# A 2-D Fourier transform feeding a SwiGLU block: another split gate, two moved ScalarE units and one later VectorE step

## The chip, the core and the metric

The kernel runs on one core of one Trainium2 chip, as one launch. The metric is the device time of one execution in microseconds (us), lower is better. A profiled execution gives a trace beside it: when each instruction of each engine started and ended. TensorE is called PE there, VectorE DVE, ScalarE ACT, GpSimd POOL and SyncE SP.

## The reference

```python
X = np.fft.fft(x, axis=1)          # x: (8, 3008, 256) float32
X = np.fft.fft(X, axis=2)
y = X.real.reshape(8 * 3008, 256)
g = y @ w_gate                     # 256 x 1536
silu = g * (1.0 / (1.0 + np.exp(-g)))
out = (silu * (y @ w_val)) @ w_out # 1536 x 256, out (24064, 256)
```

Only the real part of the transform is wanted, and x is real. So the rows k and 3008 - k of one batch come from the same two parts, one even in k and one odd: row k is even + odd, the mirrored row 3008 - k is even - odd.

## The kernel before

**Tiles and units.** The transform along the sequence gives for each batch 1504 columns of an even part (tile `Pt`) and of an odd part (`Qt`), 128 rows each; the transform along the 256 features has been multiplied into the weights at the start (`Wp` for the even part, `Wq` for the odd one, and `Wm`, which is -2 times `Wq` with its row 0 set to zero). The 12032 columns are cut into 24 tiles (`wide`: 480, 512 and 512 twice, then 512, the last one 320 and 8 columns more). A tile has 12 units, one for each 128 of the 1536 hidden columns; unit 5 of tile 17 is written (17,5). One loop (lines 1045 to 1082) runs over all 288 units, and the order in it is the order on every engine: the schedule is written out by hand, and each engine works through its own list in order.

**A unit.** The gate of the rows k is `Wp`·`Pt` + `Wq`·`Qt` in a PSUM bank g, the value the same with the value's weights in a bank v. For the mirrored rows the gate gets a third product, `Wm`·`Qt`, on top in the same bank (line 907), once ScalarE has read the bank for the first silu (`sg`, line 868). For the value, nearly all units are "split" (`split`, line 788): between the two products VectorE takes a copy `es` of the even half (line 874), and forms the mirrored value as 2·es - v (line 888, tile `VV`). Row 0 of `Qt` does not change its sign; `es` therefore has the term `bc`·`w0` in it, where `bc` is that row spread over all partitions. VectorE multiplies silu and value of the rows k (`hp`, line 882), GpSimd those of the mirrored rows (`hm`, line 912), except in units named by `on_v` (line 792), where VectorE forms the mirrored value in place (line 885) and multiplies too (line 916).

**Seeded units.** In the units of `SEED`, 1, 3 and 10, `es` costs VectorE nothing: ScalarE writes `bc`·`w0` into the v bank ahead (`seed`, line 802, instruction at line 809), the even product is added on top, ScalarE copies the sum to `es` (line 872), and the odd product uses `Wz` (`Wq` with row 0 set to zero). The seed of unit f + 1 is issued in the iteration of unit f.

**Gated units.** In the units of `GATED`, 2, from tile 4 on, the gate is split as the value is: `gate_even` (line 814) issues the even product one iteration ahead, VectorE takes `eg` = even half + `bc`·`w0` (line 823), `gate_odd` (line 827) adds the odd product and takes the silu, and one iteration later VectorE writes 2·eg - g into the bank (line 835). The product with `Wm` is not made in such a unit. There is one buffer for `eg` (`egp`, line 690).

**An iteration.** For unit u the loop issues, in this order: `part_a` (the gate's two products, the value's even product, the silu, `es`); the seed of the next unit; the waiting 2·eg - g; four of the output products (`owork`, line 770, 128x256 each, 96 to a tile, of the tile before); `gate_even` of the next unit if it is gated; `odd` of the unit before (its odd value product, `hp`, `VV`); `part_b` of the unit before (its product with `Wm`, the silu of the mirrored rows, `hm`); `gate_odd`; the copies of finished outputs to `EV` (line 730); four more output products. There are three g banks and three v banks, taken in turn, so unit f + 3 writes the bank of unit f.

**Transforms in between.** In two units of about two tiles in three (units 4 and 6, `job_at`) half of a `transform` (line 607) follows at the end of the iteration: it takes one v and one g bank aside, and VectorE writes the sums to later tiles' `Pt` and `Qt` (line 652). GpSimd folds the input for it until about tile 20. `bc` of the next tile is stored at unit 7 and loaded by DMA on SP's queue at unit 9 (lines 1032 to 1040).

```python
GATED = (2,)
SEED = (1, 3, 10)
return u[1] in ON_V.get(u[0], (8,) if u[0] < LIGHT else ())   # on_v; LIGHT = 14
return u[0] >= 4 and u[1] in GATED and split(u)               # gated
```

Of the kernel before, what the change touches and what calls it, by code (L numbers as in the profile page):

```python
# [14 lines left out]
BF16 = mybir.dt.bfloat16  # L15
AF = mybir.ActivationFunctionType
Alu = mybir.AluOpType
# [14 lines left out]
def kernel(  # L32
# [8 lines left out]
    nc = tc.nc  # L41
    B, M, D = x.shape
    Dff = moe_w_gate.shape[1]
    P = 128
# [4 lines left out]
    nF = Dff // P  # L49
    T = 512  # L50
# [23 lines left out]
    const = ctx.enter_context(tc.tile_pool(name="const", bufs=1))  # L74
# [26 lines left out]
    Wm = const.tile([P, 2, Dff], BF16, name="Wm")  # L101
# [1 line left out]
    Tab = const.tile([P, 2, 2, 2, NTAB], BF16, name="Tab")  # L103
    halfpi = const.tile([P, 1], F32, name="halfpi")
    zero = const.tile([P, 1], F32, name="zero")
    GATED = (2,)
    w0 = const.tile([P, nF + len(GATED)], F32, name="w0")
    sel = const.tile([P, P], BF16, name="sel")
    CD = const.tile([P, 2, P], BF16, name="CD")
    SDt = const.tile([P, 2, P], BF16, name="SDt")  # L110
# [1 line left out]
    mM = const.tile([P, 4], F32, name="mM")  # L112
    wC = const.tile([P, 1], F32, name="wC")
    sgn = const.tile([P, 1], F32, name="sgn")
    SEED = (1, 3, 10)
    Wz = const.tile([P, len(SEED), P], BF16, name="Wz")
    XA = const.tile([P, 8, 2, D], F32, name="XA")
    XC = const.tile([P, 8, 2, D], F32, name="XC")
    CEs = {(nm, i): const.tile([P, 2, 2, 3 * P + 1], BF16, name=f"CE{nm}{i}") for nm in "ac" for i in range(2)}
# [8 lines left out]
    Wraw = [EVw[:, i * 4 * T:(i + 1) * 4 * T].rearrange("p (n f) -> p n f", n=2) for i in range(2)]  # L128
# [123 lines left out]
    W0 = [tp.tile([P, 2, T], BF16, name=f"W0{i}") for i in range(2)]  # L252
# [52 lines left out]
    for i in range(6):  # L305
        ps = psO.tile([P, T], F32, name="o")
# [178 lines left out]
    def value_rows(fcs):  # L485

        n = T // P
        ps = psO.tile([P, T], F32, name="o")
        for fc in fcs:
            src = W0[1] if fc == 0 else Wraw[1][:, :, (fc - 1) * T:fc * T]  # L490
            for f in range(n):
                for no in range(2):
                    nc.tensor.matmul(ps[:, fc * n + f:fc * n + f + 1], src[:, no, f * P:(f + 1) * P],
                                     SDt[:, no, 0:1], start=(no == 0), stop=(no == 1))
        nc.scalar.copy(w0[:, fcs[0] * n:(fcs[-1] + 1) * n], ps[:, fcs[0] * n:(fcs[-1] + 1) * n])
        for k, f in enumerate(GATED):
            if f // n in fcs:
                src = W0[0] if f < n else Wraw[0][:, :, (f // n - 1) * T:f // n * T]
                for no in range(2):
                    nc.tensor.matmul(ps[:, nF + k:nF + k + 1], src[:, no, f % n * P:(f % n + 1) * P],  # L500
                                     SDt[:, no, 0:1], start=(no == 0), stop=(no == 1))
                nc.scalar.copy(w0[:, nF + k:nF + k + 1], ps[:, nF + k:nF + k + 1])

    psA = place(XA, putA, 4, ((psG, "g"), (psV, "v")))
    sums(SA, XA, psA)
# [37 lines left out]
    def angles_o(ch):  # L543
        t1 = rrO[:, ch].bitcast(I32)
        return [lambda i=i: vstt(rrO[:, ch, i, :], kfO, mM[:, 2 * ch + i:2 * ch + i + 1], t1[:, i, :],
                                 op0=Alu.mult, op1=Alu.subtract) for i in range(2)] + [
                lambda: magnitude(raO[:, ch], rrO[:, ch])]
# [235 lines left out]
    ON_V = {1: (6,), 2: (2, 9), 3: (2, 9)}  # L783
    LIGHT = 14

    bc = {}

    def split(u):

        return u[1] not in WHOLE.get(u[0], ())  # L790

    def on_v(u):

        return u[1] in ON_V.get(u[0], (8,) if u[0] < LIGHT else ())

    def gated(u):

        return u[0] >= 4 and u[1] in GATED and split(u)

    seeded = {}  # L800

# [12 lines left out]
    def gate_even(u):  # L814
# [6 lines left out]
        eg = egp.tile([P, T], F32, name="eg")  # L821
        k = nF + GATED.index(f)
        nc.vector.scalar_tensor_tensor(eg[:, :n], bc[t][:, :n], w0[:, k:k + 1], g[:, :n], op0=Alu.mult, op1=Alu.add)
# [11 lines left out]
        mirrored[u] = lambda: nc.vector.scalar_tensor_tensor(g[:, :n], eg[:, :n], 2.0, g[:, :n], op0=Alu.mult,  # L835
                                                             op1=Alu.subtract)

    def part_a(u):
        t, f = u
        n = width(t)  # L840
        w = n + (B if t == nT - 1 else 0)
        fs = slice(f * P, (f + 1) * P)
        if f == 0:
            hts[t] = (hp.tile([P, nF, T + B], BF16, name="hp"), hp.tile([P, nF, T], BF16, name="hm"))
        Pt, Qt = pq_tiles(t)

        def mm(ps, Wt, gv, src, start, stop):
            nc.tensor.matmul(ps[:, :w], Wt[:, gv, fs], src[:, :w], start=start, stop=stop,  # L848
                             skip_group_check=True)

        if gated(u):
            g, sg, _ = gates[u]
        else:
            g = psG.tile([P, T], F32, name="g")
            mm(g, Wp, 0, Pt, True, False)
            if u == (0, 0):
                v = psV.tile([P, T], F32, name="v")
                mm(v, Wp, 1, Pt, True, False)
            mm(g, Wq, 0, Qt, False, True)
        if split(u):  # L860
            mine = u in seeded
            e = seeded.pop(u) if mine else psV.tile()
            mm(e, Wp, 1, Pt, not mine, False)
            if not mine:
                psV.begun[id(e)] = w
            if not gated(u):
                sg = sgp.tile([P, T], F32, name="sg")
                nc.scalar.activation(sg[:, :w], g[:, :w], AF.Silu)  # L868
            stt = nc.vector.scalar_tensor_tensor
            es = next_es()  # L870
            if mine:
                nc.scalar.copy(es[:, :n], e[:, :n])  # L872
            else:
                stt(es[:, :n], bc[t][:, :n], w0[:, f:f + 1], e[:, :n], op0=Alu.mult, op1=Alu.add)  # L874

            def odd():
                if mine:
                    nc.tensor.matmul(e[:, :w], Wz[:, SEED.index(f), :], Qt[:, :w], start=False, stop=True,  # L878
                                     skip_group_check=True)
                else:  # L880
                    mm(e, Wq, 1, Qt, False, True)
                nc.vector.tensor_tensor(hts[t][0][:, f, :w], sg[:, :w], e[:, :w], op=Alu.mult)  # L882
                if on_v(u):
                    vm = e
                    stt(e[:, :n], es[:, :n], 2.0, e[:, :n], op0=Alu.mult, op1=Alu.subtract)
                else:
                    vm = next_of(VV, "vv")
                    stt(vm[:, n - 1::-1], es[:, :n], 2.0, e[:, :n], op0=Alu.mult, op1=Alu.subtract)  # L888
                state[u] = (g, vm)
            return odd  # L890
        if u != (0, 0):
            v = psV.tile([P, T], F32, name="v")
            mm(v, Wp, 1, Pt, True, False)
        psV.begun[id(v)] = w
        mm(v, Wq, 1, Qt, False, True)
        sg = sgp.tile([P, T], F32, name="sg")
        nc.scalar.activation(sg[:, :w], g[:, :w], AF.Silu)  # L897
        nc.vector.tensor_tensor(hts[t][0][:, f, :w], sg[:, :w], v[:, :w], op=Alu.mult)
        state[u] = (g, v)
# [29 lines left out]
    for b in range(2, B, 2):  # L929
        u = slot[(b, 0)] - 1  # L930
# [65 lines left out]
    job_at = {}  # L996
    for jb in jobs[1:]:
        u = slot[jb]
# [13 lines left out]
    def sine_o(ch):  # L1012
        return [lambda: sine(ch, NOO, NTAB, rrO[:, ch])]

    late = angles_o(1)
    before = {0: late[0:1], 1: weight_unit(1, 0) + late[1:2], 2: weight_unit(1, 1) + cosine_o(0), 3: late[2:3],
              4: weight_unit(2, 0), 5: weight_unit(2, 1) + cosine_o(1), 7: sine_o(0), 8: sine_o(1),
              9: [lambda: weigh(NOO, NTAB), lambda: value_rows((1, 2))],
              11: [lambda k=k, f=f: nc.scalar.activation(Wz[:, k, :], Wm[:, 1, f * P:(f + 1) * P], AF.Copy, scale=-0.5)
                   for k, f in enumerate(SEED)]}  # L1020
    loads = []

    def spread_row0(t):
# [21 lines left out]
    for i, u in enumerate(units):  # L1045
        t, f = u
        if (t, f) == (1, 0):
            spread_row0(t)
        if 0 < t < nT - 1 and f in ROW0:
            (store_row0, load_row0)[ROW0.index(f)](t + 1)  # L1050
        for fn in before.pop(i, ()):
            fn()
        run_loads(i)
        coming = part_a(u)
        if i not in job_at and i + 1 < len(units):
            seed(units[i + 1])
        if prev in mirrored:
            mirrored.pop(prev)()
        if owork:
            owork.run(4)  # L1060
        if i + 1 < len(units) and gated(units[i + 1]):
            gate_even(units[i + 1])
        if odd:
            odd()
        odd = coming
        if prev is not None:
            part_b(prev)
            if u in gates:
                gate_odd(u)
            run_evicts()  # L1070
            if prev[1] == nF - 1:
                owork = OWork(prev[0], hts[prev[0]])
                owork.run(4)
        if owork and not (prev is not None and prev[1] == nF - 1):
            owork.run(4)
        for what, j in fold_at.get(i, ()):
            fold_step(what, j, i)
        for what in act_at.pop(i, ()):
            load_next(what)
        if i in job_at:  # L1080
            transform(*job_at[i])
        prev = u
# [38 lines left out]
```

## Time and profile before

| what | value |
|---|---|
| time, median of 3 executions | 625.55 us (625.27 to 625.73) |
| time of the profiled execution | 625.21 us |
| its span, first to last instruction | 623.3 us |
| PE busy | 610.8 us (98%), 4124 matmuls recorded |
| DVE busy | 575.3 us (92%) |
| ACT busy | 470.8 us (76%) |
| POOL busy | 527.2 us (85%) |

A 128x512 matmul shows as 0.38 us, but the next one starts 0.22 us after it: ends are modelled, so starts are what is to be read on PE. Instructions of DVE and of ACT overlap a little in the same way. A few matmul records are missing; where two starts lie 0.43 apart and no row is between, one product is unseen, not a wait. In the trace's rows, an engine's idle time before an instruction, and what ended it, stands in square brackets.

### The profile page before, as it was taken

To read this page: it belongs to the slowest core of one execution; us is meant where nothing else is said; L and a number is where in the kernel's file an instruction comes from. 1 tells how busy PE (TensorE), PEld (TensorE's weight loads), DVE (VectorE), ACT (ScalarE), POOL (GpSimd) and SP (SyncE) were. 2 spreads that over 40 slices of the span, in tenths; PEclk is the share of its full clock that TensorE was granted. 3 is DMA by queue.
4 is the path that set the end of the run, shared out by engine and by line. 5 is a ranking of instruction groups with operands and counts; after the bars stand their busy time and mean duration, and the time that the engine had idled before them with its cause. 6 is when DMAs were issued, how large, how long until landed. Compare 5 with 4: busy or idle time off the path is not lost.

```text
span 623.3 us, 13287 instructions
## 1 busy us (share of the span) xinstructions
PE 610.8 (98%) x4124; PEld 396.4 (64%) x4190; DVE 575.3 (92%) x1053; ACT 470.8 (76%) x880; POOL 527.2 (85%) x543
## 2 busy tenths in 40 slices
PE   9999999999999999999999999999999999999997
PEld 6446666666666666666666666666666666666686
DVE  7889999999999999999999999999999999999991
ACT  7687868778777787787777877877787778778773
POOL 9997989899899989997997989998799856656661
PEclk9999999999999999999999999999999999999999
DMA  8682442244222253244245111134121111111112
GB/s 226 122 171 77 114 139 84 84 115 138 81 67 86 70 151 108 74 134 127 70 109 149 50 44 55 48 85 139 58 59 37 53 45 42 59 52 44 58 52 77
DMA packets 52981, 55.42 MB, mean 89 GB/s; under 512 B 7504, under 2 KB 44238, under 8 KB 52910
## 3 DMA queue, kind: packets, MB, share of 16 engines
q1 hardware_dynamic: 49726, 52.20, 29.2%
q0 software_dynamic: 3184, 2.36, 2.6%
q8 instruction: 33, 0.54, 0.4%
q14 instruction: 38, 0.31, 0.2%
HBM read 32.22 MB, written 24.67 MB: 91 GB/s over the span
## 4 chain that ended last, share of the span: by engine, by line
PE 87%; DVE 6%; ACT 3%; issue 2%; DMA 1%; SPq 0%; POOL 0%; DVEq 0%; ACTq 0%
PE o L770 37%; PE v L848 18%; PE g L848 15%; PE g L907 8%; PE v L620 2%; PE v L878 2%; DVE hp L882 2%; DVE VV L888 1%; DMA XA<-in_x_dram 1%; PE g L620 1%; ACT EV L730 1%; PE g L819 1%; ACT sg L868 1%; PE g L832 1%; DVE hm L916 1%
## 5 line engine op out<-in xcount | busy, mean ns | idle before, releaser
L912 POOL TENSOR_TENSOR hm<-sgv,VV 128x512 bf16<-128x512 f32 (+2 forms) x258 | 322.7, 1258 | 76.7 <-DVE VV L888 66.2
L911 ACT ACTIVATE sgv<-g 128x512 f32<-128x512 f32 (+2 forms) x258 | 153.7, 596 | 62.3 <-PE g L907 55.9
L882 DVE TENSOR_TENSOR hp<-sg,v 128x512 bf16<-128x512 f32 (+2 forms) x273 | 184.1, 675 | 7.6 <-PE v L848 6.2
L868 ACT ACTIVATE sg<-g 128x512 f32<-128x512 f32 (+2 forms) x253 | 151.5, 599 | 30.9 <-PE g L848 20.9
L770 PE MATMUL o<-Wo,hp 128*128 128x256 bf16 (+2 forms) x1140 | 169.6, 273 | 0.1
L770 PE MATMUL o<-Wo,hm 128*128 128x256 bf16 (+2 forms) x1140 | 169.7, 273 | 0.0
L770 PEld LDWEIGHTS <-hm 128*128 128x128 bf16 (+2 forms) x1140 | 112.0, 98 | 70.4 <-issue 2.5
L770 PEld LDWEIGHTS <-hp 128*128 128x128 bf16 (+2 forms) x1140 | 112.0, 98 | 67.8 <-issue 3.4
L888 DVE SCALAR_TENSOR_TENSOR VV<-SDf,v 128x512 f32<-128x512 f32 (+2 forms) x179 | 120.5, 673 | 0.0
L848 PE MATMUL v<-Pt,Wp 128*128 128x512 bf16 (+2 forms) x288 | 107.9, 375 | 5.2 <-DVE hm L916 0.8
L848 PE MATMUL g<-Pt,Wp 128*128 128x512 bf16 (+2 forms) x268 | 100.7, 376 | 0.1
L907 PE MATMUL g<-Qt,Wm 128*128 128x512 bf16 (+2 forms) x267 | 100.0, 375 | 0.7 <-ACT sg L897 0.7
L874 DVE SCALAR_TENSOR_TENSOR SDf<-bc,w,v 128x512 f32<-128x512 bf16 (+2 forms) x116 | 85.1, 734 | 0.2
L848 PE MATMUL v<-Qt,Wq 128*128 128x512 bf16 (+2 forms) x222 | 83.1, 374 | 0.0
L848 PEld LDWEIGHTS <-Wp 128*128 128x128 bf16 x556 | 54.2, 98 | 41.3 <-issue 7.1
L848 PE MATMUL g<-Qt,Wq 128*128 128x512 bf16 (+2 forms) x205 | 76.5, 373 | 0.0
L874 DVE SCALAR_TENSOR_TENSOR es<-bc,w,v 128x512 f32<-128x512 bf16 (+2 forms) x91 | 66.9, 735 | 0.1
L809 ACT ACTIVATE v<-bc,w 128x512 f32<-128x512 bf16 (+2 forms) x66 | 45.2, 685 | 24.1 <-DVE VV L888 23.7
L730 ACT COPY EV<-o 128x512 f32<-128x512 f32 x90 | 52.8, 586 | 4.8 <-PE o L770 4.8
L888 DVE SCALAR_TENSOR_TENSOR VV<-es,v 128x512 f32<-128x512 f32 (+2 forms) x79 | 53.2, 673 | 0.0
L848 PEld LDWEIGHTS <-Wq 128*128 128x128 bf16 x490 | 47.9, 98 | 8.0 <-issue 0.5
L872 ACT COPY SDf<-v 128x512 f32<-128x512 f32 (+2 forms) x66 | 39.1, 592 | 0.0
(189 smaller groups left out, 642.5 us busy)
## 6 DMA issues: line engine op xcount, KB each, us to landing
out_dram<-EV SPq DMA_DIRECT2D x96, 128.0 KB
XA<-in_x_dram SPq DMA_DIRECT2D x32, 256.0 KB
XA<-in_x_dram SPq DMA_DIRECT2D x112, 64.0 KB
XC<-in_x_dram SPq DMA_DIRECT2D x210, 16.0 KB
XC<-in_x_dram SPq DMA_DIRECT2D x56, 60.0 KB
bc<-row SPq DMA_DIRECT2D x20, 128.0 KB
out_dram<-EV SPq DMA_DIRECT2D x12, 120.0 KB
out_dram<-EV SPq DMA_DIRECT2D x10, 112.0 KB
```

The lines of the kernel that those rows point to most:

```text
L730: nc.scalar.copy(ev[:, 0:len(pair), :], ps[:, 0:len(pair), :])
L770: nc.tensor.matmul(ps[:n, j, :], hts[minus][:, f, c:c + n], Wo[:, f, :], start=(f == 0), stop=(f == nF - 1))
L809: nc.scalar.activation(e[:, :w], bc[t][:, :w], AF.Copy, scale=w0[:, f:f + 1])
L848: nc.tensor.matmul(ps[:, :w], Wt[:, gv, fs], src[:, :w], start=start, stop=stop, skip_group_check=True)
L868: nc.scalar.activation(sg[:, :w], g[:, :w], AF.Silu)
L872: nc.scalar.copy(es[:, :n], e[:, :n])
L874: stt(es[:, :n], bc[t][:, :n], w0[:, f:f + 1], e[:, :n], op0=Alu.mult, op1=Alu.add)
L882: nc.vector.tensor_tensor(hts[t][0][:, f, :w], sg[:, :w], e[:, :w], op=Alu.mult)
L888: stt(vm[:, n - 1::-1], es[:, :n], 2.0, e[:, :n], op0=Alu.mult, op1=Alu.subtract)
L907: nc.tensor.matmul(ps[:, :w], Wm[:, gv, f * P:(f + 1) * P], Qt[:, :w], start=False, stop=True, skip_group_check=True)
L911: nc.scalar.activation(sg[:, w - 1::-1], g[:, :w], AF.Silu)
L912: nc.gpsimd.tensor_tensor(hts[t][1][:, f, :w], sg[:, :w], v[:, :w], op=Alu.mult)
```

## The change

- Unit 0 is gated too from tile 14 on, tile 23 included: ten units. Two more one-column products at the start give its `w0` column, and all such products now stand ahead of the copies of their sums.
- Seeded units are 1, 3, 9 and 11 in place of 1, 3 and 10, in every tile from 1 on (11 not in the last tile, which is not split there). The weights of the fourth take the tile `sel`, free after tile 1 has begun.
- In the iterations that carry half of a transform, `es` of the unit is issued behind `odd` of the unit before, not ahead of it.
- `on_v` names unit 9 in place of 8 in tiles 4 to 13.

```diff
-    GATED = (2,)
+    GATED = (2, 0)
-    SEED = (1, 3, 10)
-    Wz = const.tile([P, len(SEED), P], BF16, name="Wz")
+    SEED = (1, 3, 11, 9)
+    Wz3 = const.tile([P, 3, P], BF16, name="Wz")
+    Wz = [Wz3[:, k, :] for k in range(3)] + [sel]
...
+        more = [(k, f) for k, f in enumerate(GATED) if f // n in fcs]
+        for k, f in more:
+            src = W0[0] if f < n else Wraw[0][:, :, (f // n - 1) * T:f // n * T]
+            for no in range(2):
+                nc.tensor.matmul(ps[:, nF + k:nF + k + 1], src[:, no, f % n * P:(f % n + 1) * P],
+                                 SDt[:, no, 0:1], start=(no == 0), stop=(no == 1))
         nc.scalar.copy(w0[:, fcs[0] * n:(fcs[-1] + 1) * n], ps[:, fcs[0] * n:(fcs[-1] + 1) * n])
-        for k, f in enumerate(GATED):
-            if f // n in fcs:
...
+        for k, f in more:
+            nc.scalar.copy(w0[:, nF + k:nF + k + 1], ps[:, nF + k:nF + k + 1])
...
-        return u[1] in ON_V.get(u[0], (8,) if u[0] < LIGHT else ())
+        return u[1] in ON_V.get(u[0], (9,) if u[0] < LIGHT else ())
...
-        return u[0] >= 4 and u[1] in GATED and split(u)
+        return u[0] >= 4 and u[1] in GATED[:1 if u[0] < LIGHT else 2] and split(u)
...
+    even_sums = []
-    def part_a(u):
+    def part_a(u, later):
...
-                stt(es[:, :n], bc[t][:, :n], w0[:, f:f + 1], e[:, :n], op0=Alu.mult, op1=Alu.add)
+                even_sums.append(lambda: stt(es[:, :n], bc[t][:, :n], w0[:, f:f + 1], e[:, :n], op0=Alu.mult,
+                                             op1=Alu.add))
+                if not later:
+                    even_sums.pop()()
...
-                    nc.tensor.matmul(e[:, :w], Wz[:, SEED.index(f), :], Qt[:, :w], start=False, stop=True,
+                    nc.tensor.matmul(e[:, :w], Wz[SEED.index(f)], Qt[:, :w], start=False, stop=True,
...
+    def seed_weights(k):
+        f = SEED[k]
+        nc.scalar.activation(Wz[k], Wm[:, 1, f * P:(f + 1) * P], AF.Copy, scale=-0.5)
...
-              11: [lambda k=k, f=f: nc.scalar.activation(Wz[:, k, :], Wm[:, 1, f * P:(f + 1) * P], AF.Copy, scale=-0.5)
-                   for k, f in enumerate(SEED)]}
+              11: [lambda k=k: seed_weights(k) for k in range(3)], nF + 2: [lambda: seed_weights(3)]}
...
-        coming = part_a(u)
+        coming = part_a(u, i in job_at)
...
         if odd:
             odd()
+        while even_sums:
+            even_sums.pop()()
```

More of the change, by code (lines that the diff above doesn't have):

```diff
@@ L494, in value_rows @@
                                      SDt[:, no, 0:1], start=(no == 0), stop=(no == 1))
-        nc.scalar.copy(w0[:, fcs[0] * n:(fcs[-1] + 1) * n], ps[:, fcs[0] * n:(fcs[-1] + 1) * n])
-        for k, f in enumerate(GATED):
-            if f // n in fcs:
[L498 to L502, printed above, removed]
+        more = [(k, f) for k, f in enumerate(GATED) if f // n in fcs]
[4 more added lines that the diff above has]
+                                 SDt[:, no, 0:1], start=(no == 0), stop=(no == 1))
+        nc.scalar.copy(w0[:, fcs[0] * n:(fcs[-1] + 1) * n], ps[:, fcs[0] * n:(fcs[-1] + 1) * n])
+        for k, f in more:
+            nc.scalar.copy(w0[:, nF + k:nF + k + 1], ps[:, nF + k:nF + k + 1])
     psA = place(XA, putA, 4, ((psG, "g"), (psV, "v")))
```

## The prediction

> **What bounds the kernel.** I read the page first, then the starts of TensorE's matmuls in the timeline, then, wherever two starts lie further apart than a matmul's pitch, the row that the late one waited for.
>
> ```profile
> span 623.3 us, 13287 instructions
> PE 610.8 (98%) x4124; PEld 396.4 (64%) x4190; DVE 575.3 (92%) x1053; ACT 470.8 (76%) x880; POOL 527.2 (85%) x543
> ```
>
> PE is the bound: it follows its own pitch nearly everywhere, so a product taken away is worth its pitch, and any wait put into PE's list is paid in full. VectorE, 92% busy, is close behind it, so what matters is at which unit it runs late. The start of tile 17 stands for all tiles from 14 on. Three views of it follow: PE, VectorE, ScalarE.
>
> ```profile
> 444.69 0.38 PE L878 MATMUL v<-Qt,Wz 128*128 128x512 bf16 x1
> 448.59 0.38 PE L819 MATMUL g<-Pt,Wp 128*128 128x512 bf16 x1
> 448.81 0.38 PE L848 MATMUL v<-Qt,Wq 128*128 128x512 bf16 x1
> 451.42 0.38 PE L848 MATMUL g<-Pt,Wp 128*128 128x512 bf16 x1
> 451.85 0.38 PE L848 MATMUL v<-Pt,Wp 128*128 128x512 bf16 x1
> ```
> ```profile
> 446.41 0.75 DVE L874 SCALAR_TENSOR_TENSOR SDf<-bc,w,v 128x512 f32<-128x512 bf16 x1
> 447.73 0.68 DVE L888 SCALAR_TENSOR_TENSOR VV<-es,v 128x512 f32<-128x512 f32 x1
> 449.01 0.75 DVE L823 SCALAR_TENSOR_TENSOR eg<-bc,w,g 128x512 f32<-128x512 bf16 x1 [0.60 <-PE g L819]
> 449.68 0.68 DVE L882 TENSOR_TENSOR hp<-sg,v 128x512 bf16<-128x512 f32 x1
> 450.27 0.68 DVE L888 SCALAR_TENSOR_TENSOR VV<-SDf,v 128x512 f32<-128x512 f32 x1
> 452.72 0.69 DVE L835 SCALAR_TENSOR_TENSOR g<-eg,g 128x512 f32<-128x512 f32 x1
> ```
> ```profile
> 446.68 0.69 ACT L809 ACTIVATE v<-bc,w 128x512 f32<-128x512 bf16 x1
> 447.33 0.60 ACT L911 ACTIVATE sgv<-g 128x512 f32<-128x512 f32 x1
> 447.83 0.58 ACT L730 COPY EV<-o 128x512 f32<-128x512 f32 x1
> 450.99 0.69 ACT L809 ACTIVATE v<-bc,w 128x512 f32<-128x512 bf16 x1 [0.89 <-DVE VV L888]
> ```
>
> Pitches, from neighbouring starts: PE 0.216 (448.59 to 448.81); VectorE 0.66 behind an `eg` or `es` (449.01 to 449.68), 0.60 behind `hp` and the like (449.68 to 450.27); ScalarE 0.65 behind a seed, 0.49 behind a silu. A matmul's start to its reader on VectorE is 0.42 (448.59 to 449.01). The row to remember is the last: the seed of (17,3) writes the bank of (17,0), so it waits for `VV` of (17,0), which ends at 450.95; it ends at 451.68, and the even product of unit 3 starts at 451.85, on pitch, with about 0.1 to spare. That such a seed does stop PE when it is late stands in tile 4:
>
> ```profile
> 127.93 0.69 ACT L809 ACTIVATE v<-bc,w 128x512 f32<-128x512 bf16 x1 [1.30 <-DVE VV L888]
> 128.16 0.38 PE L848 MATMUL g<-Qt,Wq 128*128 128x512 bf16 x1
> 128.67 0.38 PE L848 MATMUL v<-Pt,Wp 128*128 128x512 bf16 x1
> ```
>
> The seed ends at 128.62, the product follows 0.05 later at 128.67, where pitch would have it at 128.37: 0.30 lost.
>
> **Part 1, unit 0 gated in tiles 14 to 23.** Gone: ten products with `Wm`, nine of 0.216 and one of 320 columns (0.136): -2.08 us. Added: per tile an `eg` (0.66) and a 2·eg - g (0.60) on VectorE, against one `es` (0.66) saved by the fourth seed. What VectorE does in order, in the clock of the rows above: the new gate product takes 444.69, `eg`(0) starts 0.42 later at 445.11; `hp`(10) 445.77, `VV`(10) 446.37, `es`(0) 446.97, `hp`(11) 447.62, `VV`(11) 448.22 to 448.90. Before, that row was at 447.73 and was followed by 0.60 of idle time, the bracket at 449.01; now the lateness and the new 2·eg - g take it up. The latter also needs the silu of unit 0, which now stands on ScalarE behind the seed of unit 1 (447.08, on the end of `VV`(10) at 447.05) and the mirrored silu of 11 (447.74): 448.23 to 448.82. So 2·eg - g runs from 448.86 to 449.55.
>
> Next comes `eg`(2), and there is one `eg` buffer: it must wait for the end of 2·eg - g, which has just read it. What such a wait for the neighbour costs, the mirrored product in place shows in tile 10:
>
> ```profile
> 267.96 0.69 DVE L885 SCALAR_TENSOR_TENSOR v<-es,v 128x512 f32<-128x512 f32 x1
> 268.76 0.69 DVE L916 TENSOR_TENSOR hm<-sg,v 128x512 bf16<-128x512 f32 x1
> ```
>
> 0.80 from start to start in place of 0.60. The Trainium skill says otherwise (VectorE: DVE Perf Modes, The DRAIN you can't avoid): in a chain of vector operations "the semaphore costs nothing extra here". The row disagrees by 0.20; by the rule each of the ten starts would be 0.20 earlier, a rival below. By the row `eg`(2) starts at 449.65, `hp`(0) 450.31, `VV`(0) 450.91 to 451.59; the seed of 3 follows (0.03) 451.62 to 452.31 and PE's product (0.05) 452.36. On pitch, with one product fewer, PE would be there at 451.63: 0.73 lost in each of tiles 14 to 22, so 0.51 net. A smaller wait before it, for ScalarE's copy `es`(1), lies inside these 0.73. In tile 23 the operands of its own units are 320 columns wide; scaled by columns the chain gives about 0.4. Sum of waits 9 x 0.73 + 0.4 = +7.0.
>
> `bc` is read 1.3 earlier than at 446.41.
>
> ```profile
> 66.83 0.36 SPq L1040 DMA_DIRECT2D bc<-row  x1
> 72.02 0.75 DVE L874 SCALAR_TENSOR_TENSOR SDf<-bc,w,v 128x512 f32<-128x512 bf16 x1
> 438.73 0.35 SPq L1040 DMA_DIRECT2D bc<-row  x1
> ```
>
> Tile 2 reads it 5.2 after its issue without waiting; tile 17 now would 6.4 after. I take 0; the other end, landing only just before 446.41, would be 1.3 per tile. No DMA is added or moved.
>
> **Part 2, `es` behind `odd` in transform iterations.** At unit 4 of tiles 5, 7, 10, 13, 16 and 19 (first and last shown) PE's value product of unit 5 waits for `VV`(3), which has `es`(4) ahead of it; in tile 2 it is longer.
>
> ```profile
> 156.07 0.38 PE L848 MATMUL g<-Qt,Wq 128*128 128x512 bf16 x1
> 156.55 0.38 PE L848 MATMUL v<-Pt,Wp 128*128 128x512 bf16 x1
> 504.79 0.38 PE L848 MATMUL g<-Qt,Wq 128*128 128x512 bf16 x1
> 505.27 0.38 PE L848 MATMUL v<-Pt,Wp 128*128 128x512 bf16 x1
> 81.63 0.39 PE L848 MATMUL g<-Pt,Wp 128*128 128x512 bf16 x1
> 82.59 0.38 PE L848 MATMUL v<-Pt,Wp 128*128 128x512 bf16 x1 [0.57 <-DVE VV L888]
> ```
> ```profile
> 503.28 0.74 DVE L874 SCALAR_TENSOR_TENSOR SDf<-bc,w,v 128x512 f32<-128x512 bf16 x1
> 504.54 0.68 DVE L888 SCALAR_TENSOR_TENSOR VV<-SDf,v 128x512 f32<-128x512 f32 x1
> 510.55 1.33 DVE L652 TENSOR_TENSOR Qt<-g,od 128x160 bf16<-128x160 f32 x7 [0.34 <-PE g L641]
> ```
>
> 0.48 in place of 0.216 is 0.27, six times; tile 2 loses 0.96 - 0.43 = 0.53. The step moves `VV`(3) up by as much as 0.66, so all of it goes: -2.15. `es`(4) then runs about where `VV`(3) was, ends near 505.28, and its reader comes a good 0.3 later. PE being ahead by 0.27 afterwards is covered by the 0.34 that VectorE idles before the second half's sums; were that gone, the wait would come back there.
>
> **Part 3, seeds at 9 and 11.** The seed of 10 waits for `VV`(7), that of 9 waits for `VV`(6), nearer to the transform:
>
> ```profile
> 513.05 0.68 DVE L888 SCALAR_TENSOR_TENSOR VV<-SDf,v 128x512 f32<-128x512 f32 x1
> 514.32 0.38 PE L848 MATMUL v<-Pt,Wp 128*128 128x512 bf16 x1
> 516.05 0.38 PE L848 MATMUL g<-Qt,Wq 128*128 128x512 bf16 x1
> 516.36 0.38 PE L848 MATMUL v<-Pt,Wp 128*128 128x512 bf16 x1
> ```
>
> Before: 0.31 - 0.22 = 0.09 lost at unit 10. After: `VV`(6) ends at 513.73, the seed at 514.45, PE is let go at 514.50 and not 514.32: 0.18. About +0.1 in the seven tiles of part 2: +0.65. The seed of 11 waits for `VV`(8), in the iteration of the seeded unit 9 that leaves VectorE 0.66 free: 0. One more seed and copy per tile (0.65 + 0.49) lie in ScalarE's 24% idle; without that cover a late copy would hold the odd product by as much. At the end of tile 3 VectorE has one `es` (0.66) less to do ahead of tile 4, where it ran without a pause up to the seed at 127.93, so the 0.30 shown there goes: -0.30.
>
> **Part 4, `on_v` at 9.** In tiles 7 and 13 `hm`(8) on VectorE started 0.46 and not 0.10 behind its neighbour and held unit 11's bank:
>
> ```profile
> 369.03 0.69 DVE L916 TENSOR_TENSOR hm<-sg,v 128x512 bf16<-128x512 f32 x1 [0.46 <-ACT sg L868]
> 369.77 0.38 PE L848 MATMUL v<-Pt,Wp 128*128 128x512 bf16 x1 [0.39 <-DVE hm L916]
> ```
>
> The bracket counts 0.39 from a modelled end; I take 0.33, as VectorE was 0.36 later than its usual 0.10. Now bank 9 is held instead, wanted only by unit 0 of the next tile. VectorE's steps in that iteration, `es`(10), `hp`(9), the mirrored value, `hm`(9), take 0.66 + 3 x 0.60 + 0.20 = 2.7, some 0.7 more than PE's unit (five products of 0.216 and eight output products of half that, 1.95); the seeded unit 11 behind it takes only 1.2 and gives that back. So both go: -0.66 (at worst 0, if the delay strikes elsewhere). The rest is free: the extra column products at the start have a wait for `Qt` behind them, and one 128x128 activation hides in ScalarE's idle time.
>
> **Sum.** -2.08 + 7.0 - 2.15 + 0.65 - 0.30 - 0.66 = +2.5 on the profiled 625.21 (623.3 and 1.9 around), 627.7. That execution lies 0.34 below the median, so 628.0.
>
> **Rivals.** (a) Faster: the seed of 3 is not what ends last, because `VV`(0) keeps its old slack. Then -2.08 - 2.15 + 0.65 - 0.96 = -4.5, 621.0. It needs `VV`(0) to end by 450.87, 0.7 before my walk; it decides for a gain once the loss per tile is under about 0.45. For it speaks that the new step fits the size of the 0.60 bracket; against it that `eg`(0) first uses up most of that bracket. (b) No wait cost between neighbours, on VectorE: 9 x 0.20 less, with tile 23 some 2.0: 626.0, no change. Tile 10's row speaks against it. The section of the Trainium skill named above is for it. (c) VectorE as the bound of whole tiles: 0.60 more in ten tiles on PE's 23; the 8% idle hold this, and the seeds at 9 and 11 reset its lateness. If they didn't, 0.4 more per tile: 632. (d) The late seed spoils the next units too, or `bc` lands late in some tiles: 630.
>
> **How the numbers follow.** Forecast 0.60, a 0.14, b 0.18, d 0.06, c 0.02. About 0.2%, 1.25 us, is what a measurement can tell from no change. Leaving out a and c, and a part of d, the range is 625.2 to 630.2; the forecast's own is 626.9 to 629.2 (0.1 either way per tile). Slower 0.66, same 0.20, faster 0.14.
>
> **What would show it.** Right: in tiles 14 to 22 the value product of unit 3 starts some 0.7 behind pitch, released by the seed on ScalarE, with VectorE without idle time from `eg`(0) to `VV`(0) except for 0.1 ahead of `eg`(2); no gap at unit 4's end; 0.18 at unit 9 of the transform tiles; none at unit 10 of tiles 7 and 13. Wrong: PE on pitch at unit 3, or `eg`(2) 0.60 behind 2·eg - g.

## The result, and the profile after

The change makes the kernel slower: 629.01 us (median of 6 executions, 628.74 to 629.24) against 625.41 us for the kernel before on the same chip (624.97 to 625.80), a ratio of 1.0058 [1.0047, 1.0070]. That is 3.6 us where 2.5 were forecast.

The page of the changed kernel, first lines:

```profile
span 627.0 us, 13302 instructions
PE 610.2 (97%) x4115; PEld 394.8 (63%) x4182; DVE 574.3 (92%) x1050; ACT 492.9 (79%) x928; POOL 527.5 (84%) x543
```

The span has grown by 3.7, PE's busy time has not. So PE waits more, and the view of PE's waits says for what (columns: waited for, us in total, times, longest):

```profile
PE v L854 <- ACT v L811: 5.7, 10, 0.6
```

Line 854 is the value product (848 before), line 811 the seed (809 before): ten waits, one for each tile from 14 on. The view counts from modelled ends of matmuls; by starts these ten are 5.4 us, and with a smaller wait just ahead of them, worked out below, 6.84 us. The timeline of tile 17, on PE, VectorE and ScalarE in this order:

```profile
450.06 0.60 PE L772 MATMUL o<-Wo,hp 128*128 128x256 bf16 x4
450.66 0.38 PE L887 MATMUL v<-Qt,Wz 128*128 128x512 bf16 x1
...
451.74 0.38 PE L854 MATMUL g<-Pt,Wp 128*128 128x512 bf16 x1
452.73 0.38 PE L854 MATMUL v<-Pt,Wp 128*128 128x512 bf16 x1 [0.61 <-ACT v L811]
```
```profile
445.49 0.75 DVE L825 SCALAR_TENSOR_TENSOR eg<-bc,w,g 128x512 f32<-128x512 bf16 x1 [0.66 <-PE g L821]
...
449.20 0.69 DVE L837 SCALAR_TENSOR_TENSOR g<-eg,g 128x512 f32<-128x512 f32 x1
450.01 0.75 DVE L825 SCALAR_TENSOR_TENSOR eg<-bc,w,g 128x512 f32<-128x512 bf16 x1
...
451.27 0.68 DVE L897 SCALAR_TENSOR_TENSOR VV<-SDf,v 128x512 f32<-128x512 f32 x1
```
```profile
451.99 0.69 ACT L811 ACTIVATE v<-bc,w 128x512 f32<-128x512 bf16 x1 [0.88 <-DVE VV L897]
```

From `eg`(0) at 445.49 to `VV`(0) at 451.27 VectorE does ten steps, and the only pause in them is ahead of `eg`(2): 0.81 from start to start (449.20 to 450.01) where its neighbours need 0.60 to 0.67. `VV`(0) ends at 451.95, the seed of 3 at 452.68, and PE's product starts at 452.73. On pitch, with the one product between the last two PE rows whose record is missing, it would start at 451.74 + 2 x 0.216 = 452.17: 0.56 late. Another 0.16 was lost a little before, ahead of the odd product of unit 1, which waits for ScalarE's copy `es`(1): 450.66, where four output products from 450.06 on would let it go at 450.50. Together 0.71. The same sum over the starts of all tiles gives 0.764 in tile 14, 0.71 in each of tiles 15 to 22, 0.370 in tile 23.

The transform iterations are the second place. The wait ahead of unit 5's value product is gone; a small new one stands ahead of unit 6's gate product. Tile 16, VectorE, then PE:

```profile
430.72 0.74 DVE L880 SCALAR_TENSOR_TENSOR SDf<-bc,w,v 128x512 f32<-128x512 bf16 x1
431.38 1.32 DVE L654 TENSOR_TENSOR Pt<-g,od 128x128 bf16<-128x128 f32 x7
```
```profile
431.11 0.38 PE L854 MATMUL v<-Pt,Wp 128*128 128x512 bf16 x1
432.19 0.60 PE L772 MATMUL o<-Wo,hp 128*128 128x256 bf16 x4
432.75 0.38 PE L854 MATMUL g<-Pt,Wp 128*128 128x512 bf16 x1
```

Four output products take 0.44, so unit 6 should start at 432.63 and not at 432.75. The third place is the seed of 9 in the same tile, VectorE, ScalarE, PE:

```profile
439.00 0.68 DVE L897 SCALAR_TENSOR_TENSOR VV<-SDf,v 128x512 f32<-128x512 f32 x1
```
```profile
439.78 0.69 ACT L811 ACTIVATE v<-bc,w 128x512 f32<-128x512 bf16 x1 [0.61 <-DVE VV L897]
```
```profile
440.05 0.38 PE L854 MATMUL g<-Qt,Wq 128*128 128x512 bf16 x1
440.52 0.38 PE L854 MATMUL v<-Pt,Wp 128*128 128x512 bf16 x1
```

0.47 in place of 0.22: 0.25 lost here, and the seed starts 0.10 behind the end of `VV`(6) at 439.68.

### The profile page after: what moved, and what is told of

Read it like the earlier page. It is cut to its first block, busy times and chain, and to the rows that moved or that the text cites. A ratio compares the mean times of both kernels' runs of the same rounds, so it can differ in the third digit from the quotient of the medians.

```text
span 627.0 us, 13302 instructions
## 1 busy us (share of the span) xinstructions
PE 610.2 (97%) x4115; PEld 394.8 (63%) x4182; DVE 574.3 (92%) x1050; ACT 492.9 (79%) x928; POOL 527.5 (84%) x543
## 4 chain that ended last, share of the span: by engine, by line
PE 77%; DVE 12%; DMA 3%; ACT 3%; issue 2%; POOL 1%; SPq 0%; DVEq 0%; ACTq 0%; POOLq 0%
PE o L772 33%; PE v L854 15%; PE g L854 13%; PE g L916 7%; DVE VV L897 3%; PE v L887 3%; DVE hp L891 2%; PE v L622 2%; ACT v L811 2%; DMA XC<-in_x_dram 2%; DVE SDf L880 1%; DVE Qt L654 1%; DMA XA<-in_x_dram 1%; DVE eg L825 1%; PE g L622 1%
## 5 line engine op out<-in xcount | busy, mean ns | idle before, releaser
L874 ACT ACTIVATE sg<-g 128x512 f32<-128x512 f32 (+2 forms) x243 | 145.5, 599 | 27.4 <-PE g L854 14.7
L897 DVE SCALAR_TENSOR_TENSOR VV<-SDf,v 128x512 f32<-128x512 f32 (+2 forms) x169 | 113.6, 672 | 0.0
L854 PE MATMUL g<-Pt,Wp 128*128 128x512 bf16 (+2 forms) x258 | 96.9, 376 | 0.1
L916 PE MATMUL g<-Qt,Wm 128*128 128x512 bf16 (+2 forms) x256 | 95.9, 375 | 0.7 <-ACT sg L906 0.7
L811 ACT ACTIVATE v<-bc,w 128x512 f32<-128x512 bf16 (+2 forms) x89 | 61.2, 688 | 33.7 <-DVE VV L897 33.2
L854 PE MATMUL v<-Qt,Wq 128*128 128x512 bf16 (+2 forms) x199 | 74.5, 374 | 0.0
L854 PE MATMUL g<-Qt,Wq 128*128 128x512 bf16 (+2 forms) x195 | 72.8, 373 | 0.2 <-DVE Qt L654 0.2
L897 DVE SCALAR_TENSOR_TENSOR VV<-es,v 128x512 f32<-128x512 f32 (+2 forms) x89 | 60.0, 674 | 0.0
L880 DVE SCALAR_TENSOR_TENSOR es<-bc,w,v 128x512 f32<-128x512 bf16 (+2 forms) x69 | 50.6, 733 | 0.1
L854 PEld LDWEIGHTS <-Wq 128*128 128x128 bf16 x457 | 44.7, 98 | 8.7 <-issue 1.0
```

The costliest lines, as they stand in the source:

```text
L811: nc.scalar.activation(e[:, :w], bc[t][:, :w], AF.Copy, scale=w0[:, f:f + 1])
L880: even_sums.append(lambda: stt(es[:, :n], bc[t][:, :n], w0[:, f:f + 1], e[:, :n], op0=Alu.mult, op1=Alu.add))
L916: nc.tensor.matmul(ps[:, :w], Wm[:, gv, f * P:(f + 1) * P], Qt[:, :w], start=False, stop=True, skip_group_check=True)
```

## The experiments

All times are medians; unless said otherwise, a difference is to the changed kernel at 629.01 us, and waits are sums over PE's starts against pitch. The runs were spread over several chips, on which the kernel before took 625.07 to 625.41 us, so differences of a few tenths are read from the waits and not from the times.

**Without part 1.** Is the gate at unit 0 the loss, and all of it?

```diff
-    GATED = (2, 0)
+    GATED = (2,)
```

> The changed kernel with unit 0 not gated; parts 2, 3 and 4 stay. If the ten starts of the tiles from 14 on are the loss (0.71 us of wait at unit 3 in tiles 14 to 22 and 0.37 in tile 23, less 2.1 us of products saved), the time falls by 4.8 us, to 624.2, about 1.2 below the kernel before, and PE keeps its pitch at unit 3. If the loss lies in the other parts (seeds at 9 and 11, the later es), it stays near 629.

Measured: 624.23 us (623.94 to 625.37), ratio to the kernel before 0.9984 [0.9976, 0.9993]. So the gate at unit 0 costs 4.8 us; the other three parts together gain about 1.0. PE is on pitch at unit 3 of every tile, and the waits at unit 6 and unit 9 stay.

**A second `eg` buffer, and its control.** The pause ahead of `eg`(2) was taken for the price of waiting for the neighbour. A second buffer removes the dependence; to make room for it `sg` has three buffers and not four. The control has only the latter.

```diff
-    sgp = ctx.enter_context(tc.tile_pool(name="sg", bufs=4))
+    sgp = ctx.enter_context(tc.tile_pool(name="sg", bufs=3))
-    egp = ctx.enter_context(tc.tile_pool(name="eg", bufs=1))
+    egp = ctx.enter_context(tc.tile_pool(name="eg", bufs=2))
```

> The changed kernel with two eg buffers, and three instead of four buffers of the first silu to make room. Then eg of unit 2 needs not wait for the end of 2 eg - g of unit 0. By the row (0.80 from start to start with such a wait, 0.60 without) the wait at unit 3 falls from 0.71 to 0.51 in tiles 14 to 22, and the time by 1.9 us, to 627.1. If a wait between neighbours on VectorE costs nothing extra, nothing changes: 629.0.

> The changed kernel with three instead of four buffers of the first silu and one eg buffer: the control for the kernel with two eg buffers. Both theories expect 629.0, as a silu's buffer is read two iterations before it is written again.

Measured: 626.38 us with both (ratio to before 1.0017 [1.0008, 1.0026]), 628.38 us for the control (1.0049 [1.0037, 1.0062]). The second buffer is worth 2.00 us, ten times 0.20. Tile 17 with two buffers, VectorE and PE:

```profile
448.42 0.69 DVE L837 SCALAR_TENSOR_TENSOR g<-eg,g 128x512 f32<-128x512 f32 x1
449.02 0.74 DVE L825 SCALAR_TENSOR_TENSOR eg<-bc,w,g 128x512 f32<-128x512 bf16 x1
```
```profile
451.18 0.38 PE L854 MATMUL g<-Qt,Wq 128*128 128x512 bf16 x1
451.73 0.38 PE L854 MATMUL v<-Pt,Wp 128*128 128x512 bf16 x1 [0.17 <-ACT v L811]
```

0.60 from start to start, not 0.81, and PE's product is 0.33 late (0.55 from the row before, not 0.216); with the 0.16 at the odd product of unit 1 that is 0.50 and not 0.71. The Trainium skill (VectorE: DVE Perf Modes, The DRAIN you can't avoid) says of a chain of copies, with a semaphore behind each or only behind the last, that the semaphore costs nothing extra; for these operations the measurement decides, and it is 0.20 us for each wait on the neighbour. The control was to give the time of the changed kernel and came out 0.63 below it. Its seeds of 9 show why, VectorE and ScalarE in tile 16:

```profile
438.66 0.69 DVE L897 SCALAR_TENSOR_TENSOR VV<-SDf,v 128x512 f32<-128x512 f32 x1
```
```profile
439.38 0.69 ACT L811 ACTIVATE v<-bc,w 128x512 f32<-128x512 bf16 x1 [0.56 <-DVE VV L897]
```

The seed starts 0.03 behind the end of `VV`(6) and not 0.10. In the changed kernel this seed waits for two things, `VV`(6) on VectorE and an earlier step of ScalarE's own (by the order in the kernel its copy `od`, which empties a bank of the transform); in the control the wait on ScalarE is gone from the seed (presumably an earlier instruction has waited for that step already), and the one on VectorE is left. The wait on ScalarE had long been fulfilled, and with it the seed starts 0.06 later. PE's wait at unit 9 is 0.19 in place of 0.25 in tiles 7, 10, 13, 16 and 19.

**Unit 10 in place of unit 0.** Nine products saved where the changed kernel saves ten (tile 23 does not split its unit 10), the same two operations on VectorE, at another place.

```diff
-    GATED = (2, 0)
+    GATED = (2, 10)
```

> The changed kernel with unit 10 gated in place of unit 0 from tile 14 on: as many steps on VectorE and as many products saved (nine, since tile 23 is not split there), but the two extra steps fall into iterations 9 and 11, whose units are seeded and leave VectorE 0.66 us each. If the loss is the chain from eg of unit 0 to the seed of unit 3, it is gone and the nine products are gained: 629.0 - 6.8 - 0 = 622.2 to 622.4. If the loss is the amount of work on VectorE in these tiles, wherever it stands, the time stays near 629.

Measured: 622.40 us (622.05 to 622.76), ratio 0.9956 [0.9942, 0.9969], faster than both kernels. Tile 17, PE, at unit 3:

```profile
449.75 0.38 PE L854 MATMUL g<-Qt,Wq 128*128 128x512 bf16 x1
449.96 0.38 PE L854 MATMUL v<-Pt,Wp 128*128 128x512 bf16 x1
```

On pitch, and so is unit 10. 6.6 us lie between nearly the same work at unit 0 and at unit 10; the amount of VectorE's work over a tile is not the cause.

**Part 1 alone**, on the kernel before.

> The kernel before with part 1 alone: unit 0 gated in tiles 14 to 23, nothing else. Theory (the chain from unit 0's gate product to the seed of 3): the same wait of about 0.7 at unit 3 of tiles 14 to 22 as in the changed kernel, -2.08 + 6.8 = +4.7 us, 630 us. The seed of unit 1's 2-eg-less neighbour, the wait at unit 5 of the transform tiles and that at unit 10 stay as before. Rival (the loss lies in the seed at 9 and in parts 2 to 4, or in an interplay of the parts): within 1.3 us of the kernel before, 624 to 627 us.

Measured: 631.65 us, ratio 1.0096 [1.0082, 1.0110], so +6.2 on the kernel before where 4.7 were expected. The wait at unit 3 is there as expected (7.15 in all). But there are waits of 0.53 and 0.23 at unit 1 of tiles 14 and 16, and those at unit 5 of tiles 16 and 19 have grown from 0.27 to 0.38: -2.08 + 7.15 + 0.76 + 0.23 = +6.1. With three seeds (1, 3, 10) in place of four VectorE reaches the end of a tile later, and a gate at unit 0 finds it late.

**No seed at unit 3 from tile 14 on.** If the wait comes from the chain that ends in this seed, it should go with it.

```diff
-        if f in SEED and split(u) and psV.begun[id(psV.line[0])] >= w:
+        if f in SEED and split(u) and not (f == 3 and t >= LIGHT) and psV.begun[id(psV.line[0])] >= w:
```

> The changed kernel, but unit 3 is not seeded from tile 14 on (its es is added on VectorE, 0.66 more per tile). Theory (the chain ends in the seed of 3): the wait of 0.71 at unit 3 goes, a wait of 0.1 to 0.3 for a bank or for ScalarE's copy may stand in its place; 624 us, 625.5 at most. Rival (VectorE has too much to do in tiles 14 to 23): with 0.66 more on VectorE in ten tiles it gets slower, 629 to 635 us.

Measured: 631.85 us (631.69 to 632.07), ratio 1.0100 [1.0086, 1.0113]: 2.8 slower, as the rival had it. The wait at unit 3 is gone, all but 0.16 for the copy `es`(1). What came in its place, tile 17, VectorE, ScalarE, PE:

```profile
450.57 0.69 DVE L837 SCALAR_TENSOR_TENSOR g<-eg,g 128x512 f32<-128x512 f32 x1
451.37 0.75 DVE L825 SCALAR_TENSOR_TENSOR eg<-bc,w,g 128x512 f32<-128x512 bf16 x1
...
453.23 0.74 DVE L880 SCALAR_TENSOR_TENSOR es<-bc,w,v 128x512 f32<-128x512 bf16 x1
...
455.75 0.69 DVE L837 SCALAR_TENSOR_TENSOR g<-eg,g 128x512 f32<-128x512 f32 x1
```
```profile
456.53 0.60 ACT L920 ACTIVATE sgv<-g 128x512 f32<-128x512 f32 x1 [2.13 <-DVE g L837]
```
```profile
453.33 0.38 PE L854 MATMUL g<-Qt,Wq 128*128 128x512 bf16 x1
453.54 0.38 PE L854 MATMUL v<-Pt,Wp 128*128 128x512 bf16 x1
...
456.36 0.60 PE L772 MATMUL o<-Wo,hp 128*128 128x256 bf16 x4
457.17 0.38 PE L854 MATMUL g<-Pt,Wp 128*128 128x512 bf16 x1 [0.21 <-ACT sgv L920]
```

PE passes unit 3 on pitch and is stopped at unit 5: its gate product writes the bank of (17,2), which the mirrored silu must have read, which waits for the 2·eg - g of unit 2, and that runs late, with the `es`(3) at 453.23 ahead of it. In transform tiles it is the transform's value bank, held by a late `VV`(3):

```profile
431.02 0.33 PE L622 MATMUL v<-Tab,CEa 128*128 128x189 bf16 x2 [0.71 <-DVE VV L897]
```

So the account that the chain through the seed is the cause was too narrow. VectorE comes to unit 3 about 0.7 behind what PE needs. The seed of 3 is only where PE notices it first; it also gives VectorE 0.66 back. Without it PE is held ahead of unit 5 (0.44 to 1.15 by tile), and in tiles 14, 15, 17, 20 and 22 about 0.3 more at unit 9.

**Part 2 undone** (`es` ahead of the odd products everywhere).

```diff
-        coming = part_a(u, i in job_at)
+        coming = part_a(u, False)
```

> The changed kernel with part 2 undone alone (es ahead of the odd products everywhere). By my term of -2.15 us: 631.2 us, with the waits of 0.27 back at unit 5 of tiles 5, 7, 10, 13, 16, 19 and 0.5 in tile 2. By the trace of the changed kernel, which shows a new wait of about 0.12 at unit 6 of the same tiles (0.8 us in all): that wait goes at the same time, so the step is worth only some 1.3 us: 630.3 us. Rival (the step is worth nothing, the waits only move): 629.0 us.

Measured: 630.49 us (630.04 to 630.61), so the step is worth 1.48 and not 2.15. The old waits come back (2.28, those of tiles 16 and 19 being 0.38 and 0.33 in this company) and the new ones at unit 6 go (0.84): 1.44. Tile 16 here, VectorE, then PE:

```profile
432.12 0.68 DVE L897 SCALAR_TENSOR_TENSOR VV<-SDf,v 128x512 f32<-128x512 f32 x1
432.72 1.32 DVE L654 TENSOR_TENSOR Pt<-g,od 128x128 bf16<-128x128 f32 x7
```
```profile
432.86 0.38 PE L854 MATMUL v<-Pt,Wp 128*128 128x512 bf16 x1 [0.22 <-DVE VV L897]
434.37 0.38 PE L854 MATMUL g<-Pt,Wp 128*128 128x512 bf16 x1
```

The sums start 0.14 ahead of unit 5's value product; in the changed kernel, with `es`(4) between `VV`(3) and them, 0.27 behind it (431.38 and 431.11). They hold the bank that the transform took aside, and unit 6's gate product needs it: 1.64 from product to product with the change, 1.51 without.

**Part 3 undone** (seeds at 1, 3 and 10).

```diff
-    SEED = (1, 3, 11, 9)
+    SEED = (1, 3, 10)
```

> The changed kernel with part 3 undone alone: seeds at 1, 3, 10 (the mirrored product on VectorE stays at unit 9). By the waits themselves: the 1.9 us at the seed of 9 go, 0.56 us at unit 10 and the 0.30 of tile 4 come back: 627.9 us. By the run with unit 0 alone, which had waits of 0.53 and 0.23 at unit 1 of tiles 14 and 16 that the changed kernel has not: the seed at 11 is what keeps VectorE in time across the end of a tile, these come back too, 628.7 us or more. Rival (part 3 is needed throughout, since VectorE has one es per tile more without it): over 631 us.

Measured: 628.81 us (628.44 to 629.05), 0.20 below the changed kernel, which the times alone do not tell from no change, and close to the second value. Gone are 1.93 at unit 9; back are 0.55 at unit 10, 0.30 in tile 4, and, not in my terms, 0.66 at unit 1 of tile 14 and some 0.2 in small waits in tiles 3, 14 and 23: 0.2 less in all. Tile 14, ScalarE and PE:

```profile
371.87 0.69 ACT L811 ACTIVATE v<-bc,w 128x512 f32<-128x512 bf16 x1 [1.66 <-DVE VV L897]
```
```profile
371.74 0.38 PE L854 MATMUL g<-Qt,Wq 128*128 128x512 bf16 x1
372.61 0.38 PE L854 MATMUL v<-Pt,Wp 128*128 128x512 bf16 x1 [0.49 <-ACT v L811]
```

**Part 4 undone** (the mirrored product of unit 8 on VectorE in tiles 4 to 13).

```diff
-        return u[1] in ON_V.get(u[0], (9,) if u[0] < LIGHT else ())
+        return u[1] in ON_V.get(u[0], (8,) if u[0] < LIGHT else ())
```

> The changed kernel with part 4 undone alone: the mirrored product of unit 8, not 9, on VectorE in tiles 4 to 13. By my term of -0.66 us: the waits of 0.33 at unit 11 of tiles 7 and 13 come back, 629.7 us. Rival (with the seed at 9 the VectorE work around unit 8 is another, and the wait does not come back): 629.0 us.

Measured: 629.59 us (629.43 to 630.32), +0.58 (+0.7 in the spans), by the sum near the forecast, by the place not: no 0.33 in tiles 7 and 13, but 0.10 at unit 11 in each of tiles 4 to 13. Tile 8, ScalarE and PE:

```profile
242.79 0.69 ACT L811 ACTIVATE v<-bc,w 128x512 f32<-128x512 bf16 x1 [0.34 <-DVE hm L925]
```
```profile
243.22 0.38 PE L854 MATMUL g<-Qt,Wq 128*128 128x512 bf16 x1
243.53 0.38 PE L854 MATMUL v<-Pt,Wp 128*128 128x512 bf16 x1
```

The seed of 11 must wait for `hm`(8) when that is on VectorE. Parts 3 and 4 thus belong together: with a seed at 11, the mirrored product cannot stay at 8 for nothing.

**The gate at unit 10 from tile 4 on.** The variant that gates unit 10 was the best so far; does it carry ten tiles more?

```diff
-        return u[0] >= 4 and u[1] in GATED[:1 if u[0] < LIGHT else 2] and split(u)
+        return u[0] >= 4 and u[1] in GATED and split(u)
```

> The variant with unit 10 gated, but from tile 4 on and not from tile 14 (ten more products with Wm saved, 2.16 us; ten more 2-eg-minus-g on VectorE, where in tiles 4 to 13 it also has the mirrored product of unit 9, 0.60 more). If VectorE's backlog is absorbed by the seeded units 9 and 11 there too: 620.3 us. If a backlog of 0.6 to 0.8 is collected in each of the ten tiles: 624 to 628 us. I expect something between, 621.5 us, with waits in the transform tiles 5, 7, 10, 13 and none in 4, 8, 11.

Measured: 626.49 us (626.16 to 626.94), 4.1 slower than with the gate from tile 14. The wait stands where I had not expected it, at unit 1 of the next tile, 0.56 in each of tiles 5 to 14 (and 0.08 just ahead of it, at unit 0, whose value product writes the bank that `hm`(9) on VectorE must have read). Tile 9, VectorE, ScalarE, PE:

```profile
246.12 0.69 DVE L925 TENSOR_TENSOR hm<-sg,v 128x512 bf16<-128x512 f32 x1
246.73 0.69 DVE L837 SCALAR_TENSOR_TENSOR g<-eg,g 128x512 f32<-128x512 f32 x1
...
247.93 0.68 DVE L897 SCALAR_TENSOR_TENSOR VV<-SDf,v 128x512 f32<-128x512 f32 x1
```
```profile
248.64 0.69 ACT L811 ACTIVATE v<-bc,w 128x512 f32<-128x512 bf16 x1
```
```profile
248.60 0.38 PE L854 MATMUL g<-Qt,Wq 128*128 128x512 bf16 x1
249.38 0.38 PE L854 MATMUL v<-Pt,Wp 128*128 128x512 bf16 x1 [0.40 <-ACT v L811]
```

In these tiles VectorE has the mirrored product of unit 9 as well, and the two together are more than the seeded units 9 and 11 give back. Again `VV`(10), the seed of 1, PE: the same three steps as at unit 0, one seed further.

**Unit 10 gated, seed of 9 left out** in tiles 2, 5, 7, 10 and 13, then in all seven transform tiles and with three `sg` buffers.

```diff
-        if f in SEED and split(u) and psV.begun[id(psV.line[0])] >= w:
+        if f in SEED and split(u) and not (f == 9 and t in (2, 5, 7, 10, 13)) and psV.begun[id(psV.line[0])] >= w:
```

> The variant with unit 10 gated in place of unit 0 (622.4 us), and the seed of 9 left out in tiles 2, 5, 7, 10 and 13, where it costs 0.21 to 0.25 each by the trace (1.2 us in all). Theory (those waits are the seed's, which waits for VV of unit 6): they go, 621.2 us. Rival (part 3's seed of 9 is needed there because VectorE lacks the 0.66 that its es takes): PE waits at unit 10 or 11 in its place, 622.4 us or more.

> Unit 10 gated in place of unit 0, the seed of 9 left out in all seven transform tiles (2, 5, 7, 10, 13, 16, 19), and three sg buffers in place of four, by which most seeds lose their second wait, on a copy of ScalarE's own. From the variant with five of these tiles (621.92 us): 2 x 0.19 for tiles 16 and 19, and 0.06 at each remaining seed that PE waits for (0.2 in all): 621.3 us. Rival (without the seed at 9 in tiles 16 and 19, where unit 10 is gated, VectorE's backlog is collected at unit 10 or 11 and across the end of the tile): 622.4 to 623.5 us.

Measured: 621.92 us (621.37 to 621.99), ratio 0.9939 [0.9925, 0.9952], the fastest of all; and 622.26 us (621.67 to 622.71), 0.9951 [0.9938, 0.9965]. In the five tiles the waits of 0.21 to 0.25 go and 0.02 to 0.06 at unit 11 come, 1.0 less in all. Only 0.5 of it shows in the time; in the trace the start up to tile 1 took 0.5 longer than with unit 10 gated alone (the last section has more on it). In the second kernel tiles 16 and 19 turn against it, as its rival had it, ScalarE and PE of tile 16:

```profile
441.87 0.69 ACT L811 ACTIVATE v<-bc,w 128x512 f32<-128x512 bf16 x1 [1.24 <-DVE VV L897]
```
```profile
441.47 0.38 PE L854 MATMUL g<-Pt,Wp 128*128 128x512 bf16 x1
442.61 0.38 PE L854 MATMUL v<-Pt,Wp 128*128 128x512 bf16 x1 [0.76 <-ACT v L811]
```

Between these two products one is unseen, so 0.71 is lost at unit 11 (1.14 and not 0.43); tile 19 loses as much. Where unit 10 is gated the seed of 9 is needed. The three `sg` buffers do what they were to do: the 0.02 to 0.06 at unit 11 and the 0.02 to 0.05 at the seeds of 9 that are left are zero. The two good halves together (five tiles, three buffers) were not run.

## Why the prediction was right, and where it was not

**Part 1, right.** Forecast 0.73 in each of tiles 14 to 22 and 0.4 in tile 23, 7.0 in all; measured 0.71 and 0.37, 6.84. Every mark named for it is in the trace: the value product of unit 3, released by the seed, VectorE without a pause but for the one ahead of `eg`(2). Rival (a) is excluded by PE's wait, rival (b) by the 0.81 and by the 2.00 us that the second buffer is worth. Rival (c), VectorE as the bound of whole tiles, is excluded for these tiles by the run with unit 10 gated, which has nearly the same work. Of rival (d) nothing is seen: in tiles 17, 20 and 22, which carry no transform, PE is on pitch behind unit 3. `bc` cost nothing, as taken. Too simple was the picture that the seed of 3 is what costs: without it the loss is larger, and the gate is free at another unit. What decides is how far VectorE is behind when PE next needs it, and the price per tile is that lateness.

**Part 2, its size wrong.** The waits that were to go are gone. The step "PE being ahead by 0.27 afterwards is covered by the 0.34 that VectorE idles before the second half's sums" looked at the second half; the first half's sums stand right behind the moved `es`(4), start later against PE, and hold unit 6's gate product, 0.84 us over seven tiles. Worth -1.48 as undone, not -2.15.

**Part 3, its size wrong.** Forecast 0.18 at unit 9; measured 0.25 in five tiles, 0.21 in two, 0.10 in tile 1, 0.02 to 0.05 elsewhere: 1.93 against 0.56 before, +1.37 and not +0.65. In the seven transform tiles 0.06 of each is the second wait of the seed, which the prediction did not have. The 0.30 in tile 4 went as forecast. By the experiment that undoes it the part costs only 0.2 here, as its seeds also spare some 0.8 in tiles 14 and 23 that the gate at unit 0 would bring (which of the two, 9 or 11, does it was not separated); the prediction saw no such tie between parts.

**Part 4, right in size, in part by luck**: the 0.66 in tiles 7 and 13 is gone. But with this part undone the two waits of 0.33 do not come back; 0.10 in each of ten tiles comes in their place, behind the seed of 11. Next to the other parts, the step is thus worth its 0.6 for a reason that the prediction did not have.

**The sum.** -2.08 + 6.84 - 2.11 + 0.84 + 1.37 - 0.30 - 0.66 = +3.9; some 0.2 less in the start up to tile 1 makes it +3.7, the growth of the span. Of the 1.2 us by which the forecast growth of 2.5 was short of this, the new wait at unit 6 has 0.8 and the seed of 9 has 0.7; part 1 and the start give 0.4 back.

## What to carry to other kernels

Where one engine is the bound and a second nearly so, ask not how much work the second gets but how late it is at the next place where the first needs it: the same two operations cost 4.8 us at one unit, and at another, with the products that they save, gained 1.8. A step moved behind something is also moved ahead of something; list both, and who waits for the second. A unit that relieves an engine (here a seed) may look like the place of a loss when it is what ends it; take it away before blaming it.

## What the runs showed of the hardware

- On VectorE an instruction that waits for its neighbour starts 0.80 behind it in place of 0.60, also where the neighbour only reads what it will overwrite. Removing it ten times gave 2.00 us.
- On ScalarE a seed whose second wait is long fulfilled can start 0.06 later. In the changed kernel's trace 45 seeds find ScalarE idle. 20 of them wait for VectorE alone and 11 for VectorE and a DMA, and all 31 start 0.03 behind VectorE's end. The other 14, in tiles with a transform, wait for VectorE and for an earlier step of ScalarE's own, and start 0.10 behind. So a second wait is not always paid: in the 11 the trace has the wait for the DMA on a semaphore instruction of its own, ahead of the seed, in the 14 the one for VectorE, which comes last. That this order is the cause fits, but no run isolates it.
- Tile 1's first product starts at 47.7 us in the trace with unit 10 gated, at 48.2 and 48.8 in the two that also leave out seeds of 9, though no seed of tile 0 or 1 is touched (the last has three `sg` buffers as well). Half a microsecond of each is one VectorE step in tile 0, which scales a table (line 365). Here it is with unit 10 gated, then with five seeds of 9 left out:

```profile
42.00 0.74 DVE L365 TENSOR_SCALAR Tab<-Tab,wC 128x752 bf16<-128x752 bf16 x1
42.06 1.22 DVE L365 TENSOR_SCALAR Tab<-Tab,wC 128x752 bf16<-128x752 bf16 x1
```

In all fourteen traces this step ends 0.21 to 0.22 behind the end of the GpSimd step that runs beside it (42.53 and 43.06 here), and so takes 0.41 to 1.26 us, by when it starts. Why it is held is not shown. The other half of the 48.8 is there before 18.1 us and stays open. Each trace is one execution; differences of half a microsecond were therefore read from the tiles they concern and not from the medians alone.
